# Gated linear attention into a gated MLP: x of the first group made in place, and a shorter conversion of the weights

## The chip, the cores and the metric

One Trainium2 chip, one core of it. The metric is device time in microseconds (us) of the whole program, median over runs. A core has a matrix engine (PE; its weight loads have a row of their own, PEld), a vector engine (DVE), a scalar engine (ACT), a general engine (POOL) and a queue engine that issues the transfers (SP). Matrix products end in eight banks of PSUM; everything else is in SBUF, 128 partitions wide.

## The reference

Two stages. Attention: batch 4, 8 heads, 768 tokens, head size 48, with a state of 48 x 48 per head:

```
state = alpha[t][:, None] * state + outer(k[t], v[t])
y[t]  = q[t] @ state
```

Then y, regrouped to x of 3072 tokens x 384 channels, goes through `(sigmoid(x @ w_gate) * (x @ w_val)) @ w_out` with d_ff = 1536. All inputs are float32 values; `w_gate` is scaled by 6.92.

## The kernel before

**Tiling.** Tokens are cut into 6 groups of 512, heads into 4 pairs, so there are 24 units (group, pair), numbered u = 4 * group + pair. A pair lies on the partitions with head 0 at 0 to 47 and head 1 at 64 to 111. d_ff is cut into 12 blocks of 128, so the MLP has 72 steps s = 12 * group + block. A step is 9 matmuls for the gate, 9 for the value and 9 for the output (3 tiles of 128 channels, times 3 products: each operand is split into a high and a low part, `PAIRS`).

**A unit of the first two groups** (`unit`): two scans on DVE make the products of alpha, G backward and F forward, in chunks of 128 tokens (L381, L385). k is multiplied by G (L389) and q by F (L447); `KEYS` and `QUERIES` say for which units DVE does that, POOL has the rest. PE turns k (L402), ACT copies it out (L406), PE makes scores k.q (L459) and sums k.v (L464). DVE masks the scores into A (L472) and runs the states over four chunks (L487). POOL multiplies the states by the decay (L495). Then `outputs`: 8 matmuls from states (L506) and 8 from scores (L510), one head at a time into output partitions 0 to 47 and 64 to 111 of one bank. `finish` brings that into x, where head pairs lie densely, 96 rows each: ACT copies the bank to `yt` (L413), SP issues two or three transfers from `yt` into x (L420), and when a tile of 128 channels is complete, ACT makes its high part (L427) and DVE its low part (L429). Units of later groups go through `late` and end in the same `finish`.

**Weights** come from HBM as 8-byte floats and are converted on the chip, 25 pieces (`weight_piece`): block 0 in 3 pieces of 384 columns, blocks 1 to 11 in 2 pieces of 576. Each piece: a transfer (L340), ACT scales the upper word (L342), ACT makes the exponent part (L343), the sign is added by ACT (L346, the 13 pieces in `SIGNS`) or DVE (L349, the other 12), DVE joins the words by shift and or (L351), ACT writes the high part (L353), DVE the low part (L355).

**MLP steps** (`step`): L230 gate and value, L625 sigmoid, L627 product, L628 and L629 high and low part of h, L637 output products into three banks `po`. For steps 0 and 1, gate and value are issued in two parts, channel tiles 0 and 1, then tile 2.

**Order.** All operations are given to `Plan` with estimated durations, due times and dependences; it puts them in a fixed order per engine when the program is built (`SHIFTS` moves single due times). An engine works strictly in that order. A flag `port` marks operations that the plan keeps from running on DVE and POOL at once. `warm` adds `WARM` filler matmuls (L608, unused results) that the plan puts where PE has nothing else ready.

**Memory.** Weight blocks 6 to 11 and the second x buffer are not needed at first; `borrow` lends their space to buffers of the opening. Units 0 to 3 take three PSUM banks each from `r_bank`, a ring of seven.

Of the kernel before, what the change touches and what calls it, by code (L numbers as in the profile page):

```python
# [40 lines left out]

WIDTH = EH + 3 * T + 1
# [7 lines left out]
class Plan:  # L50
# [14 lines left out]
    def add(self, engine, time, key, fn, reads=(), writes=(), port=False):  # L65
        n = len(self.parts)
        deps = set()
        for r in reads:
            if r in self.last_write:
                deps.add(self.last_write[r])  # L70
            self.reads_since.setdefault(r, []).append(n)
        for w in writes:
            if w in self.last_write:
                deps.add(self.last_write[w])
            deps.update(self.reads_since.pop(w, ()))
            self.last_write[w] = n
        deps.discard(n)
        self.parts.append((engine, time, key, fn, deps, port or engine == "gpsimd"))

    def order(self):  # L80
# [23 lines left out]
        for _ in self.parts:  # L104
            best = None
            for e, ns in waiting.items():
# [5 lines left out]
                if e == "gpsimd" and any(self.parts[m][5] and latest[m] < latest[n] and max(free["vector"], ready_at[m]) < t + self.parts[n][1]  # L112
                                         for m in waiting["vector"]):
                    continue
# [91 lines left out]
def gla_then_glu(ctx: ExitStack, tc: tile.TileContext, q, k, v, alpha, rows, vc, vh, weights_in, out):  # L206
# [9 lines left out]
    with ExitStack() as fast:  # L216
        chunked(fast, tc, rows, vc, vh, weights_in, out, const, ident, flags, weights, within)
# [16 lines left out]
def chunked(ctx, tc, rows, vc, vh, weights_in, out, const, ident, flags, weights, within):  # L234
# [45 lines left out]
    r_v = ring("v", 2, CH, 2, D, early=[borrow("w8", CH, 2, D) for _ in range(2)])  # L280
    raws = [(f"raw{i}", sb.tile([P, WF // 2, 2], U32, name=f"raw{i}")) for i in range(2)]
    for _ in range(2):
        nm, t = borrow("w11", WF // 2, 2)
        raws.append((nm, t.bitcast(U32)))
    r_raw = Ring(raws)
    r_kn = ring("kn", 1, CH, P, early=[borrow("w6", CH, P) for _ in range(2)])
    r_yt = ring("yt", 2, T, early=[borrow("x1", T)])
# [16 lines left out]
    r_bank = Ring([*r_at.tiles, *r_po.tiles, *r_gv.tiles[1:]])  # L304
    ob = [(f"raw{i // 2}", raws[i // 2][1].rearrange("p a b -> p (a b)").bitcast(F32)[:, i % 2 * T:(i % 2 + 1) * T]) for i in range(NM)]
# [15 lines left out]

    plan.add("gpsimd", 1.2, None, later, writes=["later", *(("start", u) for u in range(EARLY))])
# [5 lines left out]
    def weight_piece(f, key):  # L328
        cuts = (0, DM, 2 * DM, WF) if f == 0 else (0, WF // 2, WF)
        over = before(f"w{f}") if f >= 6 else []  # L330
        for i, (lo, hi) in enumerate(zip(cuts, cuts[1:])):
            n = hi - lo
            rn, raw = r_raw.next() if f < NF - 1 else raws[i]
            raw = raw[:, 0:n]
            upper, lower = raw[:, :, 1], raw[:, :, 0]
            halves = raw.bitcast(U16).rearrange("p m (w h) -> p m w h", h=2)
            most, sign = halves[:, :, 0, 1], halves[:, :, 1, 1]
            ru, rl = (rn, "u"), (rn, "l")
            kk = key
            plan.add("sync", (0.475, P * n * 8 / RATE), None, lambda raw=raw, lo=lo, hi=hi: nc.sync.dma_start(  # L340
                out=raw.rearrange("p a b -> p (a b)"), in_=weights_in[f, :, 2 * lo:2 * hi]), writes=[ru, rl])
            plan.add("scalar", 0.02 + n / 960, kk, lambda up=upper.bitcast(F32): nc.scalar.activation(out=up, in_=up, func=AF.Copy, scale=2.0 ** -112), writes=[ru])  # L342
            plan.add("scalar", 0.02 + n / 960, kk, lambda most=most, lower=lower: nc.scalar.activation(  # L343
                out=lower, in_=most, func=AF.Copy, scale=2.0 ** -13, bias=2.0 ** -15 - 0.5), writes=[rl])
            if (f, i) in SIGNS:
                plan.add("scalar", 0.08 + n / 500, kk, lambda most=most, up=upper.bitcast(F32): nc.scalar.copy(  # L346
                    out=most.bitcast(F16), in_=up), [ru], [rl])
            else:
                plan.add("vector", 0.01 + n / 960, kk, lambda most=most, sign=sign: nc.vector.tensor_scalar(  # L349
                    out=most, in0=sign, scalar1=0x8000, scalar2=None, op0=ALU.bitwise_and), [ru], [rl], port=True)  # L350
            plan.add("vector", 0.07 + n / 960, kk, lambda upper=upper, lower=lower: nc.vector.scalar_tensor_tensor(  # L351
                out=lower, in0=upper, scalar=3, in1=lower, op0=ALU.logical_shift_left, op1=ALU.bitwise_or), [ru], [rl], port=True)
            plan.add("scalar", 0.02 + n / 960, kk, lambda lower=lower, lo=lo, hi=hi: nc.scalar.copy(  # L353
                out=weights.tile(f)[:, 0, lo:hi], in_=lower.bitcast(F32)), [rl], [("wh", f, i), *over])
            plan.add("vector", vec(n), kk, lambda lower=lower, lo=lo, hi=hi: nc.vector.tensor_tensor(  # L355
                out=weights.tile(f)[:, 1, lo:hi], in0=lower.bitcast(F32), in1=weights.tile(f)[:, 0, lo:hi], op=ALU.subtract),
                [rl, ("wh", f, i)], [("w", f, i)], port=True)
# [76 lines left out]
    def unit(u, g, p, t):  # L434
# [6 lines left out]
        vn, v = r_v.next()  # L441
        plan.add("sync", (0.475, P * CH * 2 * D * 4 / RATE), after(t["load"], 0.2), lambda: nc.sync.dma_start(
            out=v.rearrange("p c j e -> p (c j e)"), in_=vc[g, p]), writes=[(vn, "v")])
# [17 lines left out]
        def adds():  # L461
            for c in range(nch):
                for j in range(2):
                    nc.tensor.matmul(out=pk[R * j:R * j + D, c * D:(c + 1) * D], lhsT=kn[:, c, R * j:R * j + D], rhs=v[:, c, j],  # L464
# [17 lines left out]
        else:  # L482
            plan.add("gpsimd", 0.08, t["G"], lambda: nc.gpsimd.memset(st[:, 0, :], 0.0), writes=[sn])
# [9 lines left out]
        sdn, sd = r_vs.next()  # L493
        sd = sd[:, 0, 0:CH, :]
# [5 lines left out]
        pyn, py = pas[0] if u < NP else r_gv.next()  # L500
# [13 lines left out]
        finish(g, p, t, pyn, py)  # L514

# [96 lines left out]
    def step(s):  # L612
# [117 lines left out]
SIGNS = ((0, 0), (1, 1), (2, 0), (2, 1), (3, 1), (4, 1), (5, 1), (6, 0), (6, 1), (7, 1), (8, 1), (9, 0), (11, 0))  # L730
QUERIES = (0, 2, 5, 6)
KEYS = (0, 1, 3, 4, 5, 7)
SHIFTS = ((69, -1), (89, -2), (123, -4), (124, 2), (127, -9), (151, 24), (158, -2), (188, 22), (192, 5), (198, 20), (206, 2), (210, 1), (224, 8), (239, 12), (242, 9), (270, 2), (278, 5), (290, -7), (357, -5), (359, 15), (375, 1), (380, 3), (389, 4), (400, 4), (402, 1), (414, 21), (416, -8), (420, -7), (421, 5), (440, -3), (444, 4), (454, 2), (456, 2), (468, -5), (469, -1), (471, 5), (491, -2), (508, 6), (515, 38), (542, 5), (553, 7), (565, 4), (568, 8), (605, -10), (626, 3), (632, 3), (633, 8), (863, -1), (866, 12), (872, 7))
WARM = 60
APART = 104
# [93 lines left out]
def laid_out(np, q, k, v, alpha, w_gate, w_val, w_out):  # L829
# [17 lines left out]
    vh = vv.reshape(NG, NP, 2, EH, E, D).transpose(0, 1, 2, 4, 3, 5).reshape(NG, NP, 2, E, EH * D)  # L847
# [29 lines left out]
```

## Time and profile before

| what | value |
|---|---|
| runs | 548.3 us median of 3 (547.92 to 549.14) |
| the profiled execution | 548.93 us, its span 546.9 us, granted PE clock 0.995 |
| PE / PEld busy | 537.1 us (98%) / 433.7 us (79%) |
| DVE / ACT / POOL busy | 331.5 (61%) / 212.5 (39%) / 79.6 us (15%) |
| PE fillers | 60 |
| HBM read | 41.01 MB |

Busy PE includes the fillers. The span is from the first to the last instruction; about 2.0 us of the execution lie outside it. "Chain" below is the chain of work that ended last, followed back from the end.

### The profile page before, as it was taken

To read this page: it belongs to the slowest core of one execution; us is meant where nothing else is said; L and a number is where in the kernel's file an instruction comes from. 1 tells how busy PE (TensorE), PEld (TensorE's weight loads), DVE (VectorE), ACT (ScalarE), POOL (GpSimd) and SP (SyncE) were. 2 spreads that over 40 slices of the span, in tenths; PEclk is the share of its full clock that TensorE was granted. 3 is DMA by queue.
4 is the path that set the end of the run, shared out by engine and by line. 5 is a ranking of instruction groups with operands and counts; after the bars stand their busy time and mean duration, and the time that the engine had idled before them with its cause. 6 is when DMAs were issued, how large, how long until landed. Compare 5 with 4: busy or idle time off the path is not lost.

```text
span 546.9 us, 10258 instructions
## 1 busy us (share of the span) xinstructions
PE 537.1 (98%) x4150; PEld 433.7 (79%) x4150; DVE 331.5 (61%) x639; ACT 212.5 (39%) x386; POOL 79.6 (15%) x99
## 2 busy tenths in 40 slices
PE   8999999999999999999999999999999999999994
PEld 3767878888888888888888888888888888888883
DVE  7999899995745774546557648557556342222221
ACT  2779899863323233223223323232323222211121
POOL 2412102102202220203202112022021010000000
PEclk9999999999999999999999999999999999999998
DMA  8855787731320321402303403203311000100001
GB/s 306 284 173 182 224 258 209 235 93 63 102 79 25 102 67 37 160 18 84 103 0 103 159 1 103 86 17 102 121 41 50 1 14 16 59 0 0 2 1 64
DMA packets 22120, 51.19 MB, mean 94 GB/s; under 512 B 3504, under 2 KB 8624, under 8 KB 22064
## 3 DMA queue, kind: packets, MB, share of 16 engines
q1 hardware_dynamic: 22064, 50.46, 29.2%
q8 instruction: 34, 0.56, 0.4%
q14 instruction: 22, 0.18, 0.1%
HBM read 41.01 MB, written 4.72 MB: 84 GB/s over the span
## 4 chain that ended last, share of the span: by engine, by line
PE 96%; DMA 1%; SPq 1%; ACT 0%; issue 0%; ACTq 0%
PE gv L230 54%; PE po L637 28%; PE gv L597 3%; PE gv L402 2%; PE at L551 2%; PE gv L608 1%; DMA v<-in_vc_dram 1%; PE at L459 1%; PE at L557 1%; PE gv L506 1%; PE gv L510 1%; SPq L439 1%; PE po L459 0%; PE gv L464 0%; PE at L506 0%; PE po L506 0%
## 5 line engine op out<-in xcount | busy, mean ns | idle before, releaser
L230 PE MATMUL gv<-x,w 128*128 128x512 f32 x1296 | 315.1, 390 | 0.0
L230 PEld LDWEIGHTS gv<-x,w 128*128 128x128 f32 x1296 | 242.9, 188 | 51.1 <-issue 0.4
L627 DVE TENSOR_TENSOR gv<-gv,sg 128x512 f32<-128x512 f32 x72 | 50.5, 701 | 157.4 <-PE gv L230 150.8
L637 PE MATMUL po<-hh,w 128*128 128x512 f32 x432 | 114.1, 395 | 0.0
L628 ACT CAST hh<-gv 128x512 fp32r<-128x512 f32 x72 | 42.9, 595 | 140.3 <-DVE gv L627 133.6
L637 PEld LDWEIGHTS po<-hh,w 128*128 128x128 f32 x432 | 79.4, 188 | 17.1
L625 ACT ACTIVATE sg<-gv 128x512 f32<-128x512 f32 x72 | 43.3, 602 | 115.9 <-PE gv L230 115.9
L585 POOL TENSOR_TENSOR vs<-st,dec 64x384 f32<-64x384 f32 x32 | 35.0, 1095 | 271.7 <-DVE st L580 270.5
L629 DVE TENSOR_TENSOR hl<-gv,hh 128x512 fp32r<-128x512 f32 x72 | 49.7, 690 | 23.4 <-ACT hh L628 21.3
L637 PE MATMUL po<-hl,w 128*128 128x512 f32 x216 | 63.5, 392 | 0.0
L637 PEld LDWEIGHTS po<-hl,w 128*128 128x128 f32 x216 | 40.2, 188 | 8.4
L580 DVE SCALAR_TENSOR_TENSOR st<-st,dec,at 128x48 f32<-128x48 f32 x128 | 33.9, 265 | 4.4 <-PE at L557 0.2
L381 DVE TENSOR_TENSOR_SCAN G<-in,d1g 128x512 f32<-128x512 f32 x22 | 32.2, 1469 | 4.9 <-DMA in<-in_rows_dram 4.2
L567 DVE TENSOR_TENSOR A<-at,mask 64x256 f32<-64x256 f32 x64 | 26.9, 420 | 3.4 <-PE at L557 2.8
L389 POOL TENSOR_TENSOR in<-in,G 128x512 f32<-128x512 f32 x17 | 22.8, 1340 | 35.6 <-DVE G L381 34.8
L385 DVE TENSOR_TENSOR_SCAN F<-in,d1f 128x512 f32<-128x512 f32 x22 | 27.6, 1256 | 0.5
L538 DVE TENSOR_TENSOR A<-A,F 64x512 f32<-64x512 f32 x32 | 24.0, 750 | 0.6
L395 ACT ACTIVATE F<-F 128x512 f32<-128x512 f32 x23 | 14.7, 639 | 17.5 <-DVE A L538 14.8
L597 PE MATMUL gv<-A,vs 128*48 128x64 f32 (+1 forms) x512 | 17.6, 221 | 0.0
L597 PEld LDWEIGHTS gv<-A,vs 128*48 128x48 f32 (+1 forms) x512 | 15.2, 123 | 2.8 <-DVE A L567 2.0
L429 DVE TENSOR_TENSOR x<-x 128x512 fp32r<-128x512 f32 x18 | 12.8, 709 | 6.2 <-ACT x L427 6.2
L608 PE MATMUL gv<-ident 128*128 128x512 bf16 x55 | 15.0, 405 | 0.0
(142 smaller groups left out, 383.7 us busy)
## 6 DMA issues: line engine op xcount, KB each, us to landing
in<-in_rows_dram SPq DMA_DIRECT2D x16, 516.5 KB, 4.2
raw<-in_w_dram SPq DMA_DIRECT2D x12, 576.0 KB, 4.1
first_w<-in_w_dram SPq DMA_DIRECT2D x10, 576.0 KB, 4.7
out_dram<-raw SPq DMA_DIRECT2D x18, 256.0 KB, 2.3
v<-in_vc_dram SPq DMA_DIRECT2D x22, 192.0 KB, 4.8
A<-in_rows_dram SPq DMA_DIRECT2D x32, 128.0 KB, 3.7
x<-yt SPq DMA_DIRECT2D x35, 96.0 KB, 2.6
in<-in_rows_dram SPq DMA_DIRECT2D x4, 772.5 KB, 4.8
```

Of the source, the lines that this page charges most:

```text
L230: nc.tensor.matmul(out=dst, lhsT=lhs(a, i), rhs=rhs(b, i), start=(n == 0 and i == 0), stop=(n == len(todo) - 1 and i == NK - 1))
L381: plan.add("vector", scan(n), t["G"], lambda: nc.vector.tensor_tensor_scan(out=G[:, ::-1], data0=az[:, n:0:-1], data1=d1g[size], initial=0 ...
L385: plan.add("vector", scan(n), after(t["G"], 0.01), lambda: nc.vector.tensor_tensor_scan(out=F, data0=az[:, 0:n], data1=d1f, initial=0.0, o ...
L567: plan.add("vector", 0.43, t["mask"], lambda pa=pa, j=j, i=i: nc.vector.tensor_tensor(out=A[other[j], j].rearrange("p (c i t) -> p i c t", ...
L580: nc.vector.scalar_tensor_tensor(out=st[:, c + 1, :], in0=st[:, c, :], scalar=dec[:, c:c + 1], in1=pas[c % 2][1][:, T // 2 + c // 2 * D:T ...
L585: plan.add("gpsimd", pool_(EH * D), t["sd"], lambda j=j: nc.gpsimd.tensor_tensor(out=vs[own[j], j], in0=st[own[j], 0:EH], in1=dec[own[j]]. ...
L597: nc.tensor.matmul(out=py[R * j:R * j + D, cs], lhsT=vs[r, j, c, :], rhs=A[r, j, cs], start=True, stop=True)
L625: plan.add("scalar", act(T), first(0.3), lambda: nc.scalar.activation(out=sg, in_=got["g"][1][:, 0:T], func=AF.Sigmoid), [got["g"][0]], [sgn])
L627: plan.add("vector", vec(T), first(0.4), lambda: nc.vector.tensor_tensor(out=pv, in0=pv, in1=sg, op=ALU.mult), [sgn], [pvn])
L628: plan.add("scalar", act(T), first(0.45), lambda: nc.scalar.copy(out=hh, in_=pv), [pvn], [hhn])
L629: plan.add("vector", vec(T), first(0.5), lambda: nc.vector.tensor_tensor(out=hl, in0=pv, in1=hh, op=ALU.subtract), [pvn, hhn], [hln])
L637: nc.tensor.matmul(out=pso_now[m][1][:, 0:T], lhsT=weights.part("o", b, f)[:, m * P:(m + 1) * P], rhs=h[a][:, 0:T], start=(f == 0 and i == ...
```

## The change

Three parts, and new constants.

1. For units 0 to 3 `in_place` replaces the outputs, `yt`, the transfers and `finish`. x is made in the three `po` banks, already dense: unit p's 96 channels are three blocks of 32 rows, and each block is written by products whose left operand is 32 columns wide. For that the decayed states of both heads lie side by side in a tile whose other half is zero (two POOL operations per unit; the tiles are zeroed once), and v is loaded with a gap between the heads (`vg`). A block that holds rows of both heads gets products of both. ACT and DVE then make the high and low part of x from the bank. `r_bank` has four banks instead of seven.
2. A weight piece is loaded three half words early, from an address 6 bytes past a multiple of 8, so that the 16 top bits of each float stand in the upper half of a word. One conversion from bf16 to f16 (`most` to `high`, ACT, or DVE for the 7 pieces in `CASTS`) writes sign, exponent and four bits into the upper half of a word whose lower half was cleared once; DVE shifts and joins in place. High and low part as before.
3. Gate and value of steps 0 and 1 are issued in three parts, one for each channel tile.

`SUMS` is empty, so its branch is not used. Zeroing memsets on POOL no longer count as port users in the plan. The ring `yt` has one tile instead of three.

```diff
-    def add(self, engine, time, key, fn, reads=(), writes=(), port=False):
+    def add(self, engine, time, key, fn, reads=(), writes=(), port=None):
...
+def ahead(w, f, lo, n):
+    return bass.AP(tensor=w.tensor, offset=w.offset + f * P * WF * 4 + lo * 4 + 3, ap=[[WF * 4, P], [1, 4 * n + 4]])
...
-    r_v = ring("v", 2, CH, 2, D, early=[borrow("w8", CH, 2, D) for _ in range(2)])
+    r_vg = Ring([borrow(tag, CH, GAP) for tag in ("w8", "w8", "w6", "w6")])
+    r_v = ring("v", 2, CH, 2, D)
+    r_raw3 = Ring([])
...
+    r_raw = Ring([*raws, fourth])
+    r_top1 = Ring([("top0", sb.tile([P, WF // 2], U32, name="top0"))])
+    r_top = Ring([*r_top1.tiles, *((nm, t.bitcast(U32)) for nm, t in (borrow("w9", WF // 2), borrow("w10", WF // 2)))])
...
-    r_yt = ring("yt", 2, T, early=[borrow("x1", T)])
+    r_yt = ring("yt", 1, T)
...
-    r_bank = Ring([*r_at.tiles, *r_po.tiles, *r_gv.tiles[1:]])
+    r_bank = Ring([r_gv.tiles[1], *r_at.tiles, r_gv.tiles[2]])
...
+    for nm, t in r_top.tiles:
+        plan.add("gpsimd", 0.7, None, lambda t=t: nc.gpsimd.memset(t.bitcast(F32), 0.0), writes=[(nm, "a")], port=False)
+    for nm, t in r_vs.tiles:
+        plan.add("gpsimd", 0.4, None, lambda t=t: nc.gpsimd.memset(t.rearrange("p j c e -> p (j c e)")[:, 0:CH * 2 * D], 0.0),
+                 writes=[(nm, x) for x in range(4)], port=False)
...
-            plan.add("scalar", 0.02 + n / 960, kk, lambda up=upper.bitcast(F32): nc.scalar.activation(out=up, in_=up, func=AF.Copy, scale=2.0 ** -112), writes=[ru])
-            plan.add("scalar", 0.02 + n / 960, kk, lambda most=most, lower=lower: nc.scalar.activation(
-                out=lower, in_=most, func=AF.Copy, scale=2.0 ** -13, bias=2.0 ** -15 - 0.5), writes=[rl])
-            if (f, i) in SIGNS:
...
+            plan.add("sync", (0.475, P * n * 8 / RATE), None, lambda raw=raw, lo=lo, n=n: nc.sync.dma_start(
+                out=raw.bitcast(U16), in_=ahead(weights_in, f, lo, n)), writes=[ru, rl])
+            if (f, i) in CASTS:
+                plan.add("vector", 0.01 + n / 960, kk, lambda high=high, most=most: nc.vector.tensor_copy(out=high, in_=most), [ru], [rt], port=True)
             else:
...
+                plan.add("scalar", 0.08 + n / 500, kk, lambda high=high, most=most: nc.scalar.copy(out=high, in_=most), [ru], [rt])
+            high, low = (weights_part(f, part, lo, hi) for part in range(2))
+            word = raw[:, 0:n]
+            plan.add("vector", 0.07 + n / 960, kk, lambda lower=lower, top=top, word=word: nc.vector.scalar_tensor_tensor(
+                out=word, in0=lower, scalar=13, in1=top, op0=ALU.logical_shift_right, op1=ALU.bitwise_or), [rt, ru], [rl], port=True)
...
+    def in_place(p, t, qT, inn, vw, A, sd, st, dec):
...
+        for j in range(2):
+            r = slice(R * j, R * j + R)
+            plan.add("gpsimd", pool_(CH * D), t["sd"], lambda j=j, r=r: nc.gpsimd.tensor_tensor(
+                out=sd[r, :, D * j:D * j + D], in0=st[r, 0:CH], in1=dec[r].rearrange("p (c o) -> p c o", o=1).broadcast_to([R, CH, D]), op=ALU.mult),
+                [sn, decn], [(sdn, 2 * j), (sdn, 2 * j + 1)])
+        blocks = [divmod(3 * p + i, 4) for i in range(3)]
...
+        def from_states():
+            for c in range(CH):
+                for i in range(3):
+                    nc.tensor.matmul(out=at(i, c), lhsT=sd[0:GAP, c, 32 * i:32 * i + 32], rhs=qT[0:GAP, c * C:(c + 1) * C], start=(c == 0), stop=False)
+        def from_scores(j):
+            for c in range(CH):
+                for i, lo in (((0, 0), (1, 32)), ((2, 80), (1, 48)))[j]:
+                    nc.tensor.matmul(out=at(i, c), lhsT=vw[:, c, lo:lo + 32], rhs=A[:, j, c * C:(c + 1) * C], start=False, stop=(c == CH - 1 and (i, j) != (1, 0)))
+        plan.add("tensor", (0.9, 0.5), t["out"], from_states, [(inn, "q"), *((sdn, x) for x in range(4))], banks)
+        for j in range(2):
+            plan.add("tensor", (0.9, 0.5), t["out"], lambda j=j: from_scores(j), [(vn, "v"), (an, j), (an, 2 + j)], banks)
+        if p:
+            kk = p - 1
+            pxn, px = r_po.tiles[kk]
+            plan.add("scalar", act(T), t["y"], lambda: nc.scalar.copy(out=xin(0)[:, kk, 0], in_=px[:, 0:T]), [pxn], [("x0", kk, "h")])
+            plan.add("vector", vec(T), t["y"], lambda: nc.vector.tensor_tensor(
+                out=xin(0)[:, kk, 1], in0=px[:, 0:T], in1=xin(0)[:, kk, 0], op=ALU.subtract), [pxn, ("x0", kk, "h")], [("x0", kk, "l")])
...
-            for tiles in ([range(NK - 1), range(NK - 1, NK)] if s < 2 else [range(NK)]):
+            for tiles in ([range(k, k + 1) for k in range(NK)] if s < 2 else [range(NK)]):
...
-QUERIES = (0, 2, 5, 6)
-KEYS = (0, 1, 3, 4, 5, 7)
-WARM = 60
-APART = 104
+CASTS = ((0, 2), (3, 1), (5, 0), (5, 1), (7, 0), (7, 1), (10, 1))
+QUERIES = (0, 4, 5, 6)
+KEYS = (0,)
+WARM = 29
+APART = 24
```

`GAP` is 112. `SHIFTS` is replaced as a whole (50 entries before, 49 after). `APART` sizes an unused tile between buffers.

## Rows read from the trace of the kernel before

**Rows 1.** Busy time of each engine by stretch (start:end, length, then engines):

```profile
13.55:30.86 17.31, 17.31 (x245) 13.28 (x245) 16.62 (x38) 11.23 (x26) 5.92 (x11) 1.00 0.79 268
30.86:36.37 5.51, 4.78 (x39) 2.53 (x38) 5.19 (x11) 4.68 (x8) 0.00 (x0) 1.00 0.47 109
36.37:120.00 83.63, 83.63 (x611) 67.57 (x610) 78.71 (x136) 76.34 (x125) 12.49 (x13) 1.00 0.64 201
120.00:539.80 419.80, 419.80 (x3193) 345.07 (x3189) 221.26 (x433) 116.02 (x220) 57.58 (x58) 1.00 0.19 58
539.80:546.90 7.10, 0.01 (x1) 0.00 (x0) 0.06 (x1) 0.59 (x1) 0.00 (x0) 0.64 0.34 120
```

**Rows 2.** The same for the fillers alone (L608: PE, PEld, clock, DMA):

```profile
0.00:13.55 13.55, 9.82 (x32) 3.52 (x32) 1.00 0.84 304
13.55:30.86 17.31, 3.54 (x13) 1.05 (x13) 1.00 0.79 268
30.86:36.37 5.51, 3.78 (x17) 1.52 (x17) 1.00 0.47 109
```

**Rows 3.** Chain that ended last, opening (start, length, what):

```profile
16.45 0.44 PE gv L402 x4
16.89 1.01 PE at L506 x16
17.90 1.01 PE at L510 x16
...
21.61 1.09 PE at L459 x16
22.71 0.59 PE po L402 x4
...
24.16 0.49 PE po L464 x16
...
36.37 8.43 PE gv L230 x36
```

**Rows 4.** The same chain, outputs of a late unit:

```profile
138.79 1.03 PE gv L597 x32
```

**Rows 5.** Timeline, from the last scores to the first MLP product (start, length):

```profile
26.70 1.27 DVE L472 TENSOR_TENSOR first_w<-po,mask 128x512 f32<-128x512 f32 x2
...
30.96 0.59 ACT L413 COPY yt<-po 128x512 f32<-128x512 f32 x1 [0.87 <-ACT starts L391]
...
31.57 1.16 SPq L420 DMA_DIRECT2D x<-yt  x2
...
36.89 0.72 ACT L427 CAST x<-x 128x512 fp32r<-128x512 f32 x1
...
37.90 0.69 DVE L429 TENSOR_TENSOR x<-x 128x512 fp32r<-128x512 f32 x1
```

**Rows 6.** Timeline of DVE and POOL, four places:

```profile
9.20 0.67 DVE L389 TENSOR_TENSOR in<-in,G 128x512 f32<-128x512 f32 x1
...
25.86 0.51 POOL L495 TENSOR_TENSOR vs<-st,dec 128x192 f32<-128x192 f32 x1 [0.44 <-DVE st L487]
...
25.93 0.85 DVE L355 TENSOR_TENSOR w<-raw,w 128x384 fp32r<-128x384 f32 x1
...
33.58 0.53 DVE L355 TENSOR_TENSOR w<-raw,w 128x384 fp32r<-128x384 f32 x1
```

**Rows 7.** Groups by line and shape, 0 to 130 us (busy, mean ns):

```profile
L346 ACT CAST raw<-raw 128x576 f16<-128x576 f32 x7 | 10.9, 1551 | 0.0
...
L349 DVE TENSOR_SCALAR raw<-raw 128x576 uint16<-128x576 uint16 x5 | 4.1, 820 | 0.0
...
L389 POOL TENSOR_TENSOR first_w<-first_w,first_x 128x512 f32<-128x512 f32 x1 | 1.3, 1282 | 0.0
```

**Rows 8.** Transfers issued, 36 to 120 us (KB each, median us to landing):

```profile
raw<-in_w_dram SPq DMA_DIRECT2D x10, 576.0 KB, 4.0
...
in<-in_rows_dram SPq DMA_DIRECT2D x3, 516.5 KB, 4.5
```

More of the change, by code (lines that the diff above doesn't have):

```diff
@@ L39 @@
 EARLY = 2 * NP
+GAP = R + D
 WIDTH = EH + 3 * T + 1
@@ L77, in add @@
         deps.discard(n)
-        self.parts.append((engine, time, key, fn, deps, port or engine == "gpsimd"))
+        self.parts.append((engine, time, key, fn, deps, engine == "gpsimd" if port is None else port))
     def order(self):
@@ L205, in gla_then_glu @@
 @with_exitstack
-def gla_then_glu(ctx: ExitStack, tc: tile.TileContext, q, k, v, alpha, rows, vc, vh, weights_in, out):
+def gla_then_glu(ctx: ExitStack, tc: tile.TileContext, q, k, v, alpha, rows, vc, vh, vg, weights_in, out):
     nc = tc.nc
@@ L216, in gla_then_glu @@
     with ExitStack() as fast:
-        chunked(fast, tc, rows, vc, vh, weights_in, out, const, ident, flags, weights, within)
+        chunked(fast, tc, rows, vc, vh, vg, weights_in.bitcast(U16), out, const, ident, flags, weights, within)
     found = nc.values_load(within[0:1, 0:1], min_val=0, max_val=1)
@@ L231, in products, with chunked @@
                          stop=(n == len(todo) - 1 and i == NK - 1))
-def chunked(ctx, tc, rows, vc, vh, weights_in, out, const, ident, flags, weights, within):
+def chunked(ctx, tc, rows, vc, vh, vg, weights_in, out, const, ident, flags, weights, within):
     nc = tc.nc
@@ L351, in weight_piece @@
[L351 to L357, printed above, removed]
+            rn, raw = (r_raw if f < 7 else r_raw3).next() if f < NF - 1 else raws[i]
@@ new lines, in weight_piece @@
+            word = word.bitcast(F32)
+            plan.add("scalar", act(n), kk, lambda word=word, high=high: nc.scalar.copy(out=high(), in_=word), [rl], [("wh", f, i), *over])
+            if (f, i) in SUMS:
+                plan.add("scalar", act(n), kk, lambda low=low, word=word: nc.scalar.activation(
+                    out=low(), in_=word, func=AF.Copy, scale=-1.0), [rl, ("wh", f, i)], [("w", f, i)])
+                plan.add("gpsimd", (1.0, P * n * 8 / RATE), kk, lambda low=low, word=word: nc.gpsimd.dma_start(
+                    out=low().bitcast(F32), in_=word, accum_op=ALU.add), [rl], [("w", f, i)], port=False)
+            else:
+                plan.add("vector", vec(n), kk, lambda word=word, high=high, low=low: nc.vector.tensor_tensor(
+                    out=low(), in0=word, in1=high(), op=ALU.subtract), [rl, ("wh", f, i)], [("w", f, i)], port=True)
@@ L359, in weight, with weights_part @@
+    def weights_part(f, part, lo, hi):
+        return lambda: weights.tile(f)[:, part, lo:hi]
     def weight(nm, f):
@@ L493, in unit @@
         sdn, sd = r_vs.next()
+        if not g:
+            in_place(p, t, qT, inn, (vn, vw), (an, A), (sdn, sd), (st, sn), (dec, decn))
+            return
         sd = sd[:, 0, 0:CH, :]
@@ L847, in laid_out @@
     vh = vv.reshape(NG, NP, 2, EH, E, D).transpose(0, 1, 2, 4, 3, 5).reshape(NG, NP, 2, E, EH * D)
+    vg = np.zeros((NP, C, CH, GAP), np.float32)
+    for j in range(2):
+        vg[..., R * j:R * j + D] = vc[0].reshape(NP, C, CH, 2, D)[..., j, :]
     w = np.empty((NF, P, 3, DM), np.float64)
```

68 lines of the change are left out of this document (40 added, 28 removed).

## The prediction

> **What bounds the kernel now.** I read the busy time by stretch first [rows 1], then the fillers [rows 2], then the chain and the timeline of the opening [rows 3, 5]. The reader is to see that PE has no gap between 36.37 us, the first MLP product, and 539.80, the last: 83.63 busy of 83.63, then 419.80 of 419.80, at a granted clock of 1.00, which is the 2.4 GHz level. Behind that lie 7.10 us in which the last output is copied and stored. So whatever ACT or DVE save after 36.37 buys nothing by itself. What can be gained is the time ahead of 36.37 in which PE does no work of use: of its busy time there, 9.82 + 3.54 + 3.78 = 17.1 us are fillers [rows 2]. The end of the program moves by as much as the point moves at which PE has left the opening behind, and back by all work that PE is given in addition.
>
> The last part of the opening is a wait for x. The masks of unit 3 end at 27.97 and its outputs at 30.86, where the stretch of rows 1 ends; then `yt` is copied (30.96), SP issues two transfers (31.57), ACT makes the high part only at 36.89, and the low part ends at 38.59 [rows 5]. PE meanwhile runs 17 fillers, 3.78 us.
>
> **The change part by part.**
>
> *Products in place.* Removed per unit: 8 matmuls from states and 8 from scores. In the trace a float32 matmul stands as two records, so this is 16 records in 1.01 us twice, 63 ns each, 2.02 us [rows 3]. Added: 4 chunks x 3 blocks = 12 matmuls from states and 4 x 4 = 16 from scores, 24 and 32 records. The trace has no product with a left operand of 32 columns. From above: if a record keeps the 63 ns, 56 x 63 = 3.5 us. From below: a late unit's outputs, 64 columns long instead of 128, take 1.03 us for 32 records, 32 ns each [rows 4], 1.8 us for 56, less than is removed. I take 63 ns where two strips of the array alternate, as they did before (scores, 2.02 us), and two thirds of it where three do (states, 24 x 42 ns = 1.01): 3.03 us a unit, 1.0 more than now, 4.0 over four units.
>
> The Trainium skill ("TensorE: Matmul & The Clock Gate", Part 3: Packing small matmuls) has a rule against this: a weight load overlaps with running matmuls only if its row group differs. All new products use the same rows. But so do the products of L510, and 16 of their records took 1.01 us [rows 3], no more than those of L506 with two row groups. The trace does not follow the rule here; by the rule, records would lie at least as far apart as in the second rival, which has its price from a row.
>
> *The way to x.* Gone are `yt`, ten transfers of SP and the wait for them. Left behind the last product: one ACT copy (0.59 for the like one in rows 5) and one DVE difference (0.69). They take 1.3 us where the old way took 38.59 - 30.86 = 7.7. They also need no cover of fillers, as products of tiles 0 and 1 can now go first: their x needs units 0 to 2 only, each tile of a gate or value is 3 matmuls, and 36 matmuls took 8.43 us, 0.23 each [rows 3], so gate and value over two tiles are 2.8 us of work for PE.
>
> *When the opening ends.* The scores of the first unit begin at 13.55, where the stretch of rows 1 begins. Before them DVE multiplies k of unit 1 at 9.20 (0.67 us) [rows 6]; that goes to POOL, so I take 13.0. From there PE has: turning of units 2 and 3, 0.44 + 0.59; their sums, 2 x 0.49; four scores of 1.09, 4.36 [rows 3]; four outputs of 3.03, 12.12. Together 18.5 us, to 31.5 if nothing is waited for. Before, the same list with 2.02 is 14.4 in 17.31 us, the rest being 13 fillers: DVE was the bound there (16.62 busy of 17.31). DVE is not later now: unit 3's masks ended at 27.97, three of its multiplications of k and q in units 0 to 3 (0.6 each) go to POOL, two passes for the value weights (0.53 for the one in rows 6) must come in earlier. So masks by about 27.5, one half of the last score products behind them by 28.5, and PE's own 31.5 is later. PE takes DVE's place as the bound of this stretch. Then unit 4's turning and sums, 0.44 + 0.49: at 32.4 PE is where it was at 36.37. Gain 36.37 - 32.4 = 4.0 us.
>
> *POOL and the shared port.* Keys of units 1, 3, 4, 5 and 7 move from DVE (0.67) to POOL (1.28) [rows 6, 7]; the memsets run in POOL's idle start. Beside a POOL multiplication of 0.51, a DVE difference of 0.85 stands that takes 0.53 alone [rows 6], so the two do wait for each other: a move saves DVE 0.6 us or costs it up to 0.7. In the opening this is covered by DVE's operations on PSUM (masks and states), and by PE's being later; at worst two such moves, 1.4 us, are still inside the 3 us that DVE now has to spare. I count nothing, and let the fast case below gain from it.
>
> *Weights.* Per piece ACT loses two passes; signs on ACT were 1.55 us each, on DVE 0.82 [rows 7]. The new conversion has no row; from the one side it costs what DVE's sign pass does, 0.82, from the other what ACT's with its two-byte output does, 1.55; I take 1.55, the nearer form. At 1.55 for the 18 pieces on ACT, ACT still has less than before (13 x 1.55 and 50 passes removed), and it was 76.34 of 83.63 busy [rows 1]. DVE has 12 sign passes fewer and 7 conversions more, 5 x 0.82 = 4 us less of 78.71. All of this is beside a PE that is full, so it is worth nothing in itself; it pays for the weights being due 4 us earlier. If that cover were gone, each us by which a block is late is a us of PE.
>
> *Smaller.* `r_bank` has four banks for twelve uses where it had seven: a unit's scores must wait until an earlier unit's masks or states have been read out. DVE works the units nearly in turn, so I take no cost, and up to 1 us of waiting in PE, with the later products queued behind it. SP is rid of ten transfers in the opening and has the same loads left, so none is later. One `yt` instead of three: units 4 to 23 are over 10 us apart, nothing. There are 31 fillers fewer: before, 32 ran by 13.55, so 29 last nearly to the first scores, and behind these PE has real work without a break; no clock is lost.
>
> **Sum.** Against the profiled execution: 548.93 - 4.0 = 544.9, span 542.9. The median of the runs shown is 0.6 lower than that execution, so for the median 548.3 - 4.0 = 544.3 us.
>
> **Rivals.**
>
> 1. *The opening becomes quicker than that* (24%): outputs cost 2.6 us a unit or less, and DVE, freed of three multiplications, brings everything forward. With 1.8 us a unit PE would end at 26.6, so DVE bounds: last score products at 28.5, then 0.9, gain 7.0; up to 1.8 us more where POOL hides its work fully. For it: DVE has gaps in the opening, POOL is busy for only 5.92 of 17.31 us [rows 1]. Against it: three engines in turn for each unit. Time 541 us.
> 2. *The strips do not overlap* (9%), the one that ends slower. Place: the outputs of units 0 to 3, PE the bound. A float32 product of 128 columns that shares nothing with its neighbour is the turning, 0.44 / 4 = 110 ns a record [rows 3]; 56 x 110 = 6.2 us a unit, the opening ends at 13.0 + 6.4 + 24.6 + 0.9 = 44.9, 8.5 later than now: 556.8 us. It decides from (36.37 - 0.93 - 13.0 - 6.4) / 56 / 4, 72 ns a record. Against it: two strips do overlap in L510.
> 3. *Outputs as dear as the upper bound, or waits for banks* (12%): 63 to 72 ns a record, 3.5 to 4.0 us a unit, gain 2.0 down to 0: 546.3 to 548.3 us.
> 4. *The new loads are slow* (7%), slower too. Every row of a weight piece now begins 2 bytes off a word. From 36 to 120 us the DMA engines are 0.64 busy [rows 1], about half of the whole being weights (22 pieces of 0.59 MB of the 16.8 MB that 201 GB/s move in 83.63 us are 77%, 0.49). If such a row took twice the time the share would be 1.13, the weights would bound, and about 11 us are lost: 555 us; it turns the sign from 1.75 times on, where 0.15 + 0.49 x 1.75 reaches 1. Against it: the rows of `in_rows` have 6180 bytes and start at any word, yet 516.5 KB land in 4.5 us where 576 KB of weights take 4.0 [rows 8].
>
> **How the numbers follow.** The forecast, a gain of 2.5 to 5.5 us, has 48%: 544.3, its own range 542.8 to 545.8. Range for 8 in 10: down to 540.5, which leaves most of rival 1 in, and up to 548.0, which leaves out rivals 2 and 4 and the end of 3. About 0.2% (1.1 us) is what a measurement of this kernel tells from no change. Faster: 48 + 24 + half of rival 3, 78%; same 7%; slower 15%.
>
> **What would show it.** Right: the first MLP product before 30 us and PE without a gap from about 32 on; the last masks near 27 to 28; no transfer from `yt` before 45 us; new outputs near 1 us for each 16 to 24 records; some 18 ACT conversions of 0.7 to 1.6 us. Wrong: records of the new outputs 70 ns apart or more; a granted clock below 1.00 between 13 and 32 us, where the 1.2 GHz level would double 18 us of PE; PE idle before weights between 40 and 120 us; landing times of the weight loads well over 5 us.

## The result, and the profile after

552.85 us median of 5 runs (551.39 to 553.53) against 548.52 for the kernel before (547.92 to 549.23): ratio 1.0067, 95% interval 1.0053 to 1.0080. The change makes the kernel slower, by 4.3 us between the medians and 2.9 to 4.4 by the interval; the forecast was 544.3, faster by 4. The profiled execution took 552.85 us, its span 551.0, granted PE clock 0.993.

First the busy time by stretch of the kernel after (start:end, length, then PE, PEld, DVE, ACT, POOL, PEclk, DMA share, GB/s), as in [rows 1]; PE's last product ends at 543.9 where it ended at 539.8:

```profile
13.55:30.86 17.31, 16.34 (x266) 12.78 (x257) 13.99 (x35) 7.60 (x17) 11.78 (x12) 1.00 0.64 229
30.86:36.37 5.51, 5.51 (x66) 4.25 (x65) 5.51 (x8) 2.21 (x4) 2.14 (x4) 1.00 0.48 161
36.37:120.00 83.63, 80.59 (x539) 63.75 (x538) 75.21 (x132) 47.69 (x86) 13.79 (x14) 0.98 0.62 197
120.00:543.90 423.90, 423.90 (x3269) 348.35 (x3268) 224.56 (x435) 117.35 (x222) 58.68 (x58) 1.00 0.18 57
```

The reader is to see two things. POOL is busy for 11.78 us of the opening where it was 5.92, and PE has gaps there. And between 36.37 and 120, where PE had been full for 83.63 us, it is busy for 80.59 at a clock of 0.98. Behind that PE is full in both, at the same rates (nine output products take 2.04 us in both), and the longer last row is work that was still left at 120: the 4.1 us are all lost before about 125. ACT did get lighter (47.69 for 76.34), as forecast.

The chain that ended last, in the opening of the kernel after (start, length, what), against [rows 3]:

```profile
19.53 1.21 DVE first_x L410
...
20.89 1.85 POOL first_w L480
...
22.95 1.27 POOL first_w L414
...
25.31 1.07 PE po L571 x22
...
26.88 1.87 PE po L576 x32
...
32.94 1.87 PE po L576 x32
...
38.16 5.70 PE gv L236 x24
```

L571 and L576 are the new outputs, 24 and 32 records in 1.0 and 1.87 us. Before unit 2's outputs the chain leaves PE: DVE's scan F, POOL's product of q with it (L480), POOL's k of the next unit (L414), and then its decayed states, on which L571 waits. Unit 3's masks end only at 32.10 (31.42 and 0.68 in the timeline of DVE) and its outputs at 34.81.

The opening is held up from its start by PE's own fillers. From the timeline (start, length), k of unit 0 on DVE, the first turning and the first scores:

```profile
5.18 0.66 DVE L414 TENSOR_TENSOR in<-in,G 128x512 f32<-128x512 f32 x1
...
3.69 3.62 PE L681 MATMUL gv<-ident 128*128 128x512 bf16 x8
7.11 0.81 PE L427 MATMUL gv<-ident,in 128*128 128x128 f32 x4
...
10.39 1.16 PE L492 MATMUL at<-in 48*128 48x128 f32 x16
```

This k is there at 5.84, but thirteen fillers stand ahead of the turning in PE's fixed order, 0.43 us apart up to 7.11; later ones stand 0.21 apart. In the kernel before the turning waits for DVE (0.22 us), and the fillers hold nothing up. When the spacing goes from 0.43 to 0.21 differs from one execution to the next: at 5.8 us in e1 and e3 below, which have the same thirteen fillers, and at 4.4 in e2. The first turning then begins at 6.43, 6.45 and 6.17, and in e3 and e2 the rest of the opening, which is that of the kernel after, is earlier as a whole: unit 3's outputs end at 33.96 and 33.74. So up to 1.1 us of a difference between two traces can lie here and not in an edit.

At 38.16 PE has done unit 4's turning and sums and 12 MLP products. The kernel before was there at 36.37 + 12 x 8.43 / 36 = 39.2 [rows 3]. So the kernel after leads by 1.0 us, and not by 4.0. Then it loses 5. First, the conversion of the third piece of weight block 0, the output weights of steps 0 and 1, from the timeline (start, length):

```profile
46.20 0.38 DVE L363 CAST first_w<-first_w 128x384 f16<-128x384 bf16 x1
...
47.07 0.55 DVE L368 SCALAR_TENSOR_TENSOR first_w<-first_w,first_w 128x384 uint32<-128x384 uint32 x1
47.65 0.51 ACT L371 CAST w<-first_w 128x384 fp32r<-128x384 f32 x1 [0.92 <-DVE first_w L368]
...
48.21 3.20 PE L710 MATMUL po<-hh,w 128*128 128x512 f32 x6 [0.86 <-ACT w L371]
48.31 0.55 DVE L378 TENSOR_TENSOR w<-first_w,w 128x384 fp32r<-128x384 f32 x1
```

PE has no other work by then and waits 0.86 us for ACT's high part, after 0.77 and 0.55 in the short work of unit 5 just before. And the six output products then take 3.20 us; late in the run nine take 2.04, so six 1.36. The granted clock says why (PE busy, PEclk, DMA share, GB/s):

```profile
38.00:44.00 6.00, 6.00 (x35) 1.00 0.27 87
44.00:48.00 4.00, 2.03 (x35) 1.00 0.39 103
48.00:49.00 1.00, 0.68 (x2) 0.74 0.84 342
49.00:51.00 2.00, 2.00 (x5) 0.50 0.71 194
51.00:52.00 1.00, 1.00 (x4) 0.55 0.88 360
```

After a stretch in which PE was busy for 2.03 of 4.00 us the clock stands at 0.50, the 1.2 GHz level, until about 51.9: 0.68 x 0.26 + 2 x 0.50 + 0.45 = 1.6 us lost.

Where PE's time went, summed from the starts of successive rows of its timeline to the point where PE has done the same products in all three, 120.9 us before, 124.8 after and 122.3 in e6a (us):

| PE's time | before | after | e6a, below |
|---|---|---|---|
| fillers | 16.2 | 9.4 | 8.3 |
| outputs of units 0 to 3 | 8.0 | 12.3 | 12.1 |
| waits between groups | 1.2 | 3.8 | 3.0 |
| turning, scores, sums | 17.0 | 18.1 | 17.5 |
| output products of the MLP | 22.4 | 24.0 | 22.5 |
| gate and value, 199 products | 45.8 | 46.9 | 48.2 |

After against before: -6.8, +4.3, +2.6, +1.1, +1.6 (the clock), and +1.1 for gate and value, 0.7 of it in short groups (3 products in 0.89 us, 36 in 9.1 for 8.43). Together 3.9, which is 124.8 - 120.9.

The rest of the prices: conversions by line and shape (busy, mean ns), and the weight loads from 36 to 120 us (KB, median us to landing), against [rows 7, 8]; the last line is of the kernel before and stands beside the 4.0 of [rows 8]:

```profile
L365 ACT CAST top<-raw 128x576 f16<-128x576 bf16 x6 | 5.2, 859 | 1.8 <-DVE first_w L368 1.5
...
L363 DVE CAST top<-raw 128x576 f16<-128x576 bf16 x3 | 1.5, 496 | 0.0
...
raw<-in_w_dram SPq DMA_DIRECT2D x12, 577.0 KB, 4.8
first_w<-in_w_dram SPq DMA_DIRECT2D x7, 577.0 KB, 4.5
...
first_w<-in_w_dram SPq DMA_DIRECT2D x8, 576.0 KB, 4.7
```

### The profile page after: what moved, and what is told of

It is laid out like the page before. It is cut to its first block, busy times and chain, and to the rows that moved or that the text cites. A ratio compares the mean times of both kernels' runs of the same rounds, so it can differ in the third digit from the quotient of the medians.

```text
span 551.0 us, 10327 instructions
## 1 busy us (share of the span) xinstructions
PE 538.3 (98%) x4215; PEld 435.3 (79%) x4215; DVE 328.7 (60%) x629; ACT 179.2 (33%) x337; POOL 93.8 (17%) x113
## 4 chain that ended last, share of the span: by engine, by line
PE 96%; DVE 1%; POOL 1%; issue 0%; ACT 0%; POOLq 0%; ACTq 0%
PE gv L236 54%; PE po L710 28%; PE gv L670 3%; PE gv L427 2%; PE at L624 2%; PE gv L681 1%; PE at L630 1%; PE po L576 1%; PE at L492 1%; PE gv L542 1%; PE gv L546 1%; PE po L571 1%; PE gv L497 0%; POOL first_w L480 0%; PE po L681 0%
## 5 line engine op out<-in xcount | busy, mean ns | idle before, releaser
L710 PE MATMUL po<-hh,w 128*128 128x512 f32 x432 | 115.8, 399 | 1.0 <-ACT w L371 0.9
L658 POOL TENSOR_TENSOR vs<-st,dec 64x384 f32<-64x384 f32 x32 | 36.4, 1139 | 277.1 <-DVE st L653 261.5
L702 DVE TENSOR_TENSOR hl<-gv,hh 128x512 fp32r<-128x512 f32 x72 | 49.6, 689 | 24.5 <-ACT hh L701 22.4
L414 POOL TENSOR_TENSOR in<-in,G 128x512 f32<-128x512 f32 x21 | 28.7, 1367 | 39.3 <-DVE G L406 33.0
L406 DVE TENSOR_TENSOR_SCAN G<-in,d1g 128x512 f32<-128x512 f32 x22 | 34.1, 1551 | 2.1 <-DMA in<-in_rows_dram 2.1
L611 DVE TENSOR_TENSOR A<-A,F 64x512 f32<-64x512 f32 x32 | 23.4, 731 | 0.5
L431 ACT COPY kn<-gv 128x512 f32<-128x512 f32 x21 | 12.3, 586 | 12.2 <-PE gv L427 10.0
L438 ACT COPY yt<-gv 128x512 f32<-128x512 f32 x20 | 11.7, 586 | 11.7 <-PE gv L670 7.4
```

Source lines behind the costliest of these rows:

```text
L406: plan.add("vector", scan(n), t["G"], lambda: nc.vector.tensor_tensor_scan(out=G[:, ::-1], data0=az[:, n:0:-1], data1=d1g[size], initial=0 ...
L414: plan.add(e, vec(n) if u in KEYS else pool_(n), t["kt"], lambda: getattr(nc, e).tensor_tensor(out=kT, in0=kT, in1=G, op=ALU.mult), [gn, ( ...
L658: plan.add("gpsimd", pool_(EH * D), t["sd"], lambda j=j: nc.gpsimd.tensor_tensor(out=vs[own[j], j], in0=st[own[j], 0:EH], in1=dec[own[j]]. ...
L702: plan.add("vector", vec(T), first(0.5), lambda: nc.vector.tensor_tensor(out=hl, in0=pv, in1=hh, op=ALU.subtract), [pvn, hhn], [hln])
L710: nc.tensor.matmul(out=pso_now[m][1][:, 0:T], lhsT=weights.part("o", b, f)[:, m * P:(m + 1) * P], rhs=h[a][:, 0:T], start=(f == 0 and i == ...
```

## The experiments

In the moves below `(n, m)` puts operation n of the plan behind operation m on the fixed order; all else stays as it was planned.

**e1: q of units 1 to 3 on DVE**, and unit 1's scores ahead of four fillers. On the kernel after. Of these q the change had moved only unit 2's to POOL.

```diff
-            plan.add(e, ..., lambda: getattr(nc, e).tensor_tensor(out=qT, in0=qT, in1=F, ...
+            plan.add(e, ..., lambda: getattr(nc, "vector" if u in (1, 2, 3) else e).tensor_tensor(out=qT, in0=qT, in1=F, ...
+MOVES = ((73, 69), (103, 99), (133, 129), (77, 62))   # q behind its scan F; scores of unit 1 ahead of four fillers
```

> The changed kernel with its order kept; q of units 1 to 3 is multiplied on DVE right behind its scan instead of on POOL, and unit 1's scores go ahead of four fillers. Theory (POOL's q waits for DVE to let go of the shared port and delays each unit): the last outputs of unit 3 end near 32.8 us instead of 34.8, total 551 us; the stop of PE at 44 to 52 us stays. Rival (PE itself bounds the opening, as predicted): end of the outputs moves by less than 0.7 us and the total stays at 552.9.

550.66 us, 1.0043 (1.0030 to 1.0057), 2.2 less than after by the medians, 1.3 by the two ratios. POOL in the kernel after (first two rows), then POOL and DVE in e1:

```profile
20.88 2.10 POOL L480 TENSOR_TENSOR first_w<-first_w,first_x 128x512 f32<-128x512 f32 x1 [2.36 <-DVE dec L412]
22.95 1.27 POOL L414 TENSOR_TENSOR first_w<-first_w,G 128x512 f32<-128x512 f32 x1
```

```profile
20.95 1.27 POOL L420 TENSOR_TENSOR first_w<-first_w,G 128x512 f32<-128x512 f32 x1 [3.51 <-issue]
```

```profile
18.92 0.69 DVE L486 TENSOR_TENSOR first_w<-first_w,first_x 128x512 f32<-128x512 f32 x1
```

The q product costs DVE 0.69 us, at once behind its scan. On POOL it took 2.17 and 2.10 us in units 1 and 2, where it begins beside DVE's next scan (20.71 to 21.93 for unit 2), and 1.68 in unit 3, beside a DVE difference of 0.55; k came behind it. The last outputs end at 32.92 in e1, 1.9 us earlier, as expected, but 0.9 of that is the earlier first scores (9.51 for 10.39), which the edit does not touch. From the first scores to the last outputs e1 takes 23.4 us for 24.4: 1.0 us is the edit's. The two parts of it are not told apart. The four fillers stand at 16.10 to 17.06 in the kernel after, ahead of unit 1's scores, though POOL's q was there at 16.25; so up to 0.8 us may be theirs. What is shown is that the round through POOL and the place of these fillers cost 1.0 us together. The stop at 48 us stays (PE clock 0.83 from 44 to 54).

**e3: the waits filled.** Twelve fillers in the three waits from 43 to 48 us.

```diff
+    plan.also = {344: [fill] * 4, 291: [fill] * 3, 347: [fill] * 5}
```

> The changed kernel with twelve more fillers on PE in the three waits between 43.7 and 48.2 us (4, 3 and 5). Theory (the 1.2 GHz stretch at 48.6 to 51.9 follows from the waits, and costs 1.7 us by itself): the clock stays at 1.00, total 551.2 us, 1.2 to 1.7 less. Rival (the stretch comes from elsewhere or costs nothing because DVE is late anyway): total 552.9 or more.

551.64, 1.0059 (1.0045 to 1.0073): by the medians 1.2 less than after, by the ratios 0.4, with intervals that overlap. From 49 to 51 us the row is now:

```profile
49.00:51.00 2.00, 1.74 (x8) 1.00 0.82 242
```

The wait for the weights is still there, but no slow stretch. In the traces e3 leads by 0.85 us already at the end of unit 3's outputs, ahead of the edit, and by 1.3 at the end (span 549.7 for 551.0). So the clock that is kept is worth some 0.5 us there, not the 1.6 that the slow stretch took from PE: step 2's gate, which begins at 52.00 in the kernel after, begins at 50.31 and has waited 0.26 us for its weights. That the time came out as expected is in part luck.

**e2: the third piece of block 0 converted early**, and three output products of step 0 ahead of unit 5's turning.

```diff
+MOVES = ((164, 175), (165, 164), (166, 165), (167, 335), (311, 322), (312, 311), (313, 312))
```

> The changed kernel; only four operations that convert the third piece of weight block 0 are moved up, from 46 to 49 us to about 36 to 39 us, and the first three output products of step 0 stand ahead of unit 5's turning on PE. Theory (PE stops at 44 us because that piece comes last, and falls to 1.2 GHz for it): idle of PE between 43.7 and 49 us falls from 2.3 us to under 1, the granted clock stays at 1.00, total 549 us (3.5 to 4 less). Rival (DVE has too much to do there, the order does not matter): the stop only moves elsewhere, total within 1 us of 552.9.

553.45 (551.11 to 554.13), 1.0102 (1.0087 to 1.0117): not better. Its runs lie in two groups: two at 551.1 and 551.7 with a mean granted clock of 0.998, four at 553.4 to 554.1 with 0.990 to 0.995. The profiled execution, the quickest, has the clock at 1.00 and no wait at the output products; PE's longest wait is another:

```profile
PE gv L242 <- ACT w L377: 2.5, 1, 2.5
```

It stands at 50.45, at the gate of step 2: block 2's first piece is not converted. The expectation failed, and its rival held: one piece brought forward only shows the next one late.

**e4: e1 and e2 together.**

```diff
+MOVES = (those of e1, those of e2)
```

> e1 and e2 together on the kernel after: q of units 1 to 3 on DVE, and the third piece of block 0 converted early. If the opening and the stop at the first output products were the whole loss, the two gains add: 547 us or less. If the supply of weights is late as a whole (the first part of block 2 is converted only at 49 to 51 us in e2), the opening's gain of 2 us turns into a longer wait ahead of step 2 and the time stays at 550 to 552.

553.18, 1.0071 (1.0049 to 1.0092). The gains don't add: unit 3's outputs end 1.2 us earlier (33.59), PE waits 2.55 us at 50.81, and the clock is 0.87 from 44 to 54. The rival's wait is there, but the time is over both expectations, by the clock: two of the six runs took 551.2 at a mean clock of 0.998, four 553.1 to 554.3 at 0.990 to 0.993.

**e5: and the first pieces of blocks 2 and 3 change places** in the order of conversion; block 3's had come first.

```diff
+MOVES += ((179, 189), (189, 356), (180, 190), (190, 294), (181, 191), (191, 357), (182, 192), (192, 358), (198, 208), (208, 195))
```

> e4 with one thing more: the first parts of weight blocks 2 and 3 change places in the order of conversion on ACT and DVE (block 2's was converted after block 3's, though step 2 comes first and its load had landed). Theory (what is lost behind the opening is the order in which pieces are converted, not the work of converting them): the wait ahead of step 2 goes, PE is full from about 34 us, granted clock 1.00, and the time is 545 to 547, faster than before. Rival (ACT and DVE can't supply more): the wait only moves to the next piece, 549 to 551.

550.40, 1.0039 (1.0027 to 1.0050), 2.8 less than e4 by the order of two pieces. Most of that is the clock: against e4's two runs that kept it 0.8 us are left. Step 2's gate begins at 47.18 without a wait, the clock is 1.00 from 34 us on, and nine of the ten runs have a mean of 0.996 to 0.998. The expected 545 to 547 did not come, as what PE still waits for is:

```profile
PE gv L242 <- DVE st L526: 1.4, 1, 1.4
PE gv L242 <- ACT sg L704: 1.2, 1, 1.2
PE gv L503 <- ACT kn L437: 0.7, 1, 0.7
PE po L716 <- ACT hh L707: 0.3, 1, 0.3
```

The time is the rival's (549 to 551), but no weight piece is among these waits: order again, a state behind a scan on DVE, a sigmoid behind a conversion on ACT.

**e6a and e6: these waits moved against**, and in e6 three more pieces brought forward.

```diff
+MOVES += ((335, 299), (167, 299), (340, 335), (341, 340), (289, 304), (362, 360))   # e6a
+MOVES += ((194, 326), (195, 194), (196, 189), (183, 193), (184, 196), (185, 192), (186, 185), (197, 358), (187, 338))   # e6
```

> e5 with three groups of operations moved against its three remaining waits of PE (1.39 us at 38.93 for DVE's states of unit 4, 0.73 at 35.39 for ACT's copy of the turned k, 1.18 at 53.31 for ACT's sigmoid behind a weight conversion): the scan of unit 5 behind those states, the turning of unit 4 one product group earlier, the sigmoid ahead of the conversions. Theory (what the kernel after loses to before is waits of PE that the order makes; PE itself has about 5 us more work and 8.7 us fewer fillers): each us of wait that goes is a us of time, 547.5 to 548.5, level with before or just under it. Rival (the weights of steps 2 and 3 are due too early for ACT, DVE and the loads): the third wait only turns into one for a weight piece, 549 to 550.

> e6a and, in addition, the three weight pieces that are due next ((3,1), (3,0), (2,1)) brought forward into idle time of DVE and ACT between 45 and 50 us, the load of (2,1) ahead of two others. Theory: no wait of PE of over 0.3 us after 34 us; 546.5 to 547.5, faster than before by 0.2 to 0.35%. Rival (supply is short): a later piece is late by as much, 549 or more.

e6a: 549.79, 1.0021 (1.0012 to 1.0030). e6: 550.73, 1.0035 (1.0021 to 1.0049). The waits of e6a:

```profile
PE po L716 <- ACT hh L707: 0.8, 1, 0.8
PE gv L503 <- ACT kn L437: 0.6, 1, 0.6
PE at L498 <- DVE in L486: 0.5, 1, 0.5
PE gv L242 <- DVE st L526: 0.5, 1, 0.5
PE gv L242 <- ACT w L377: 0.4, 1, 0.4
```

Of the 3.6 us in e5 2.8 are left, cut in five, and 0.6 us were won (1.0 by the ratios). That fits with each us of wait being a us of time, but is too small to show it, and the expected 547.5 to 548.5 did not come: these moves mostly spread the waits. In e6 one of 1.7 us came back (a sigmoid behind the conversions brought forward), and its expectation failed too. None of these versions beats the kernel before; e6a is 1.1 us behind it.

**e0, e0b, e0c: the conversion alone, and the place of two tiles.** e0 is the kernel before, its order unchanged, with the new conversion, on ACT for 13 pieces and DVE for 12 as the signs were, and loads 2 bytes past a multiple of 8 (6 in the kernel after); the tile that this needs takes its room from a `yt` tile and the spacer. e0b is e0 with the spacer so long that `hh` and `hl`, the tiles behind it, keep their old addresses. e0c is the kernel before with them 64 bytes lower.

```diff
-APART = 104
+APART = 24    # e0, with the new conversion
+APART = 40    # e0b, with the new conversion
+APART = 88    # e0c, nothing else
```

> The kernel before, its order of operations kept one for one; only the conversion of the weights is the new one (two ACT passes a piece left out, the sign pass replaced by the bf16 to f16 conversion on the same engine, rows loaded from 2 bytes past a multiple of 8; one yt tile fewer to make room). Theory (the conversion is harmless, PE is full after 36 us): 548.5 us, within 0.8 of before, ACT some 35 us less busy, weight loads land in 4 to 5 us. Rival (the new loads or the new conversion delay the weights): 551 us or more, PE idle before weights between 36 and 120 us.

> The kernel before with the new conversion alone, as in e0, but with the unused spacer 16 words a row longer, so that hh and hl (the left operands of the output products) lie at the very addresses that they had before. Theory (in e0 PE lost its 6 us by the place of hh and hl, 64 bytes from the old one, not by the conversion): 548.5 us, no difference to before within 0.2%, nine late products in 2.04 us again. Rival (the new conversion, its loads or its writes slow every product): 554 to 555 us, nine products in 2.06 (gate, value) and 2.10 (output) as in e0.

> The kernel before with nothing changed but the spacer, 16 words a row shorter, so that hh and hl lie 64 bytes lower, as in e0. Theory (place alone): 554 us, ratio 1.010 to 1.012, output products at 2.10 us for nine. Rival (the conversion did it): 548.3, no difference.

e0 554.60, 1.0124 (1.0108 to 1.0139); e0b 548.50, 1.0002 (0.9993 to 1.0012); e0c 554.42, 1.0107 (1.0090 to 1.0125). In e0 PE waited for nothing after 36 us, so its 6 us looked like a price of the conversion; it was the place. A late step of e0c in the chain:

```profile
300.81 2.06 PE gv L230 x9
302.87 2.10 PE po L637 x9
```

and of the kernel before:

```profile
298.65 2.04 PE gv L230 x9
300.69 2.04 PE po L637 x9
```

So the conversion by itself is worth nothing, as forecast. The kernel after does not pay for the place: nine of its output products take 2.04 us.

**e7: x in place alone**, with the old conversion at the new one's places in the order.

```diff
-                plan.add("scalar", ..., lambda high=high, most=most: nc.scalar.copy(out=high, in_=most), [ru], [rt])
+                plan.add("scalar", ..., passes, [ru], [rt])   # two scaling passes on ACT, then the sign
```

> The kernel after with the weights converted as before (aligned loads, two more ACT passes a piece, sign on ACT or, for the seven pieces in CASTS, on DVE), each at the place of the new conversion in the order: x in place alone. Theory (the weights are on the path since x in place makes them due earlier, so ACT's passes count here though they counted for nothing in the kernel before): six pieces stand between 36 and 54 us, each with 1.5 us more of ACT (two passes of 0.75) and 0.7 to 0.9 more for the sign, and the waits of PE at the first output products and ahead of step 2 grow by 2 to 4 us each: 556 to 560 us. Rival (the stop is made by the order alone, with ACT at hand): ACT was 47.7 of 83.6 us busy, the extra passes fit in its idle time, 552.5 to 554.

570.70, 1.0396 (1.0382 to 1.0409), 17.9 us more than after, far beyond both expectations. Busy time by stretch, and PE's longest waits:

```profile
44.00:54.00 10.00, 6.16 (x45) 4.13 (x43) 7.01 (x14) 7.11 (x13) 0.03 (x1) 0.76 0.42 128
...
60.00:70.00 10.00, 7.37 (x42) 5.48 (x41) 5.55 (x9) 9.57 (x15) 0.00 (x0) 1.00 0.69 237
...
100.00:120.00 20.00, 19.20 (x109) 14.81 (x107) 15.65 (x27) 15.00 (x23) 3.17 (x3) 0.83 0.59 177
```

```profile
PE po L723 <- ACT hh L714: 3.6, 2, 1.9
PE po L723 <- ACT w L384: 2.5, 1, 2.5
...
PE gv L236 <- ACT yt L451: 1.7, 1, 1.7
```

PE waits 14.2 us from 34 to 141, mostly for ACT (9.57 of 10 busy from 60 to 70), and the clock falls twice. The shorter conversion is worth nothing in the old order and some 18 us in the new. What is not told apart: an order planned for the longer passes might lose less.

**e8: gate and value of steps 0 and 1 in two parts**, as before.

```diff
-lambda b, i: xin(g)[:, i, b, :], tiles),
+lambda b, i: xin(g)[:, i, b, :], tiles if s >= 2 or tiles[0] == 2 else range(2 * tiles[0])),
```

> The kernel after with the third part of the change undone: gate and value of steps 0 and 1 in two parts (tiles 0 and 1 together, at the place where tile 1's products stood). Theory (PE is the bound in the opening, these products only move): no difference to after beyond 0.5 us, 552.4 to 553.3. Rival (tile 0's products are what covers PE while unit 3's masks are made): PE waits up to 2 us near 29 us in their place, 554 to 555.

552.89, 1.0073 (1.0052 to 1.0094), beside 552.85 after. The median is as expected by luck, for no run is near it: three took 551.3 to 551.7 at a mean clock of 0.996 to 0.998, three 554.1 to 554.9 at 0.991. The traces say more, as the first scores begin at 10.39 in both. Unit 3's last outputs in e8, from its chain:

```profile
33.63 1.87 PE po L576 x32
```

They end at 35.50 for 34.81, since PE stands idle near 29 us where the products of tile 0 had been. So the third part wins some 0.7 us in the opening, the rival's mechanism at a smaller price; what of it reaches the end the times don't tell.

## Why the prediction was wrong, step by step

**New outputs: right.** 3.03 us a unit were forecast; 12.3 / 4 = 3.07 came with waits, 2.88 in units 0 and 1 without. The states' 24 records took 1.01, as chosen, the scores' 32 took 1.87 for 2.02, 58 ns each. That ends rival 2 (110 ns a record) and the dear outputs of rival 3; a wait for a bank shows in none of PE's rows. The Trainium skill's rule ("TensorE: Matmul & The Clock Gate", Part 3: Packing small matmuls), that a weight load overlaps only another row group, was left out of the sum and is not borne out by these records, which share their rows and stand 42 and 58 ns apart.

**New loads: right enough.** 4.8 and 4.5 us to land against 4.0 [rows 8] and 4.7; with the aligned loads of e7, 3.9 and 3.7. Rival 4 wanted twice the time; PE waited for none directly. Its 22 pieces were 18 (10 and 8 are issued in that stretch), a share of 0.40 and not 0.49, so the rival was less likely than its sum made it.

**"To 31.5 if nothing is waited for ... PE takes DVE's place as the bound": failed.** The first scores began at 10.39 and not at 13.0. The 18.5 us of the list, with unit 1's turning and sums (1.08) that now stand behind them, would have ended at 30.0; unit 3's outputs ended at 34.81. Of the 4.8 us between, 1.8 are six products of gate and value done ahead, which is no loss, 1.6 are fillers (0.65 and 0.97) and 1.4 waits; 0.73 more come before unit 4's sums. "Masks by about 27.5" failed by 4.6 us: they ended at 32.10. The bound of this stretch was neither PE's work nor DVE but PE's first fillers, to which no cost was given, and behind them the round DVE, POOL, PE.

**POOL moves, "still inside the 3 us that DVE now has to spare. I count nothing": failed.** The allowance was made for DVE waiting for POOL. What waited was POOL: a product of 1.28 us took 2.1 to 2.2 beside a DVE scan, k stood behind it in a row, and PE waited 0.85 us for q (at 23.04) and then for what came behind k. e1 gave back 1.0 us of the opening, together with the place of four fillers. The Trainium skill ("SBUF — State Buffer", SBUF: two separate sides) says that of DVE with two SBUF inputs and GpSimd the later one stands still for the whole instruction of the other. The rows agree nearly: POOL's 2.10 us are 20.88 to the scan's end at 21.93 and 1.05 more, a little less than the 1.28 that the product takes alone.

**Weights, "worth nothing in itself; it pays for the weights being due 4 us earlier": the first half is right (e0b), the second failed.** The sum of ACT's and DVE's work was in fact less; I read the busy time of a whole stretch and not the order in which pieces come. Block 0's third piece had landed by about 20 us and was converted at 46 to 49, and block 2's first piece stood behind block 3's. e2, e4 and e5 show the chain of these: each earlier piece shows the next, and with two of them in the order of need PE no longer waits for either. e7 shows how near to the bound ACT comes with the old passes once the weights are due early. The new conversion itself was taken at 1.55 us and took 0.86 on ACT.

**"No clock is lost": failed.** The sign named for it was the stretch from 13 to 32 us, where the granted clock stayed at 1.00; it fell at about 48.5, behind waits that were not forecast. PE lost 1.6 us in the slow stretch; what comes back without it is 0.5 in the traces of e3, and 2 to 3 us lie between the runs of e2, e4 and e8 with and without it.

**The gain's size.** The forecast lead of 4.0 us was 1.0 at 38.16. Even without any new wait the account is 6.8 us of fillers saved against 4.3 of outputs and 0.7 of short groups: 1.8 us, not 4.0. The old opening's 17.1 us of fillers [rows 2] were not all to be had, since 29 of them still took 9.4, the first thirteen 5.5. No rival of mine had the mechanism that decided; one of the signs of being wrong (PE idle before weights between 40 and 120 us) is what came.

## What to carry to other kernels

Work that is hidden in one order is not hidden in another: price a part of a change under the order it will have, since the shorter conversion was worth nothing here alone and 18 us together with the earlier start. Fillers in a fixed order are work like any other: count those that stand ahead of each first step. Where the start of a full engine is brought forward, list what each of its first steps needs and when that is made, operation by operation; a share of busy time over 80 us says nothing on it. Before an edit is credited with a difference between two traces, see that they agree up to the edit. And keep the addresses of tiles fixed when a size is changed for a test, or the place is measured and not the edit.

## What the runs showed of the hardware that was not expected

- 64 bytes in the place of `hh` and `hl` cost 6 us (e0c, 1.0107): nine output products take 2.10 us for 2.04, and nine of gate and value 2.06, though x and the weights that these read are allocated elsewhere and not behind the spacer. Why, no run here shows.
- Waits of 2 us in a stretch of 4 were followed by 3.3 us at the 1.2 GHz level; twelve fillers there kept the clock at 1.00 (e3). A wait of 2.5 us was followed by a slow stretch in the trace of e4 (0.62 and 0.53 from 51 to 55 us) and by none in that of e2.
- PE's first fillers stood 0.43 us apart, then 0.21; the spacing changed at 4.4 us in one execution (e2) and behind 7.1 in another (the kernel after). The row of the granted clock says 1.00 throughout; why, no run here shows.
- A conversion from bf16 to f16 with steps in its rows took 496 ns on DVE and 859 on ACT for 128 x 576; DVE's 16-bit sign pass had taken 820 [rows 7].
